# Attention and SoLU kernel, first stage: sums of squares as Gram products, low words shifted by ScalarE, the first strided values loaded to both places

## The chip, the cores and the metric

The kernel runs on one core of a Trainium2 chip. The metric is the device time of one execution in microseconds (us); lower is better. Of the kernel before, the median of three runs is 548.46 us (547.02 to 554.54). One further execution was recorded with the hardware profiler: it took 552.05 us, and its span, from which all times "at x us" below are counted, is 550.3 us.

## The reference

An attention over 8 batches of 8 heads, 576 positions and 64 channels, and behind it a SoLU layer (512 to 1024 to 512) on the 4608 tokens.

```python
mask_local = (rel >= 0) & (rel < 32)                               # heads 0 to 3
mask_strided = (rel >= 0) & (pos[None] % 32 == pos[:, None] % 32)  # heads 4 to 7
attn = softmax(where(masks, q @ k.T / sqrt(64), -1e9)) ; x = attn @ v
h = x @ w_in                                       # 4608x512 @ 512x1024
solu = h * softmax(h)
ln = (solu - mean(solu)) / sqrt(var(solu) + 1e-6) * g_ln
return ln @ w_out                                  # 4608x1024 @ 1024x512
```

`q`, `k`, `v` and `g_ln` are 32-bit floats; `w_in` and `w_out` arrive as 64-bit floats, that is as two 32-bit words for each number.

## The kernel before, in words

**Attention.** Each batch has five units: two of the strided heads (`UNITS` 0 and 1; the positions are laid out so that each residue modulo 32 is a block of 18) and three of the local heads. A unit `n` makes scores on TensorE (L385 adds the mask by a product with the unit matrix, L390 is q times k), takes maximum, difference, exponential and sum (L396 to L400), scales with the reciprocal on GpSimd (L408), splits the result into two half-precision parts in `p` (L414 on ScalarE, L415 on VectorE), turns `p` by a DMA transpose into `pt` (L417) and multiplies with the values (L439) into `x_ps`. The product is again split into two parts, `xhi` and `xlo` (L455, L456), rings that hold two batches.

**Values.** `vloc` and `vstr` of a batch are loaded (L322) and their squares summed by ScalarE (`v_scale`, L329). A product with ones (L298) adds over the partitions, and from the total a power of two is made (L302 to L308, in `pow2_scale`). `v_split` (L344, L345) makes two half-precision parts; seven DMAs (L360) copy them to where the products need them, four of them for the strided values (`vd`, in both halves of the partitions) and three for the local ones (`ve`).

**Weights.** Once, ahead of the layer: `decode` loads a piece of 512 numbers of a weight row (L565), takes the high word through ScalarE (Prelu, L568), shifts the low word right by 29 on VectorE (L571) and joins the two (L572). There are 16 such pieces, 8 of `w_in` and 8 of `w_out`. ScalarE sums their squares (L584, L605), `pow2_scale` makes a scale, and each weight is split into two half-precision parts: for `w_in` the upper one by ScalarE (L591), the lower one by TensorE (a product with `wdiag`, L595, less one with `minus`, L597) and a copy (L599); for `w_out` by L618 and L619.

**Layer.** A token tile is 128 tokens, 36 in all. `ff` has two halves of the first product, each of 12 matmuls of 512 columns (`g1`, L497 to L499, into `h_ps`), then maximum (L504), exponential (L515), product (L518), centring (L522, L523), squares (L525), a short chain on GpSimd (L529 to L533), a DMA transpose of `c` into `ct` (L536), and two halves of the second product (`g2`, L541 to L543). The result goes out by L549 and L550.

**Order.** Every step is given to `Plan.add` with its engine, an assumed duration, what it reads and writes, and a key. `Plan.order` simulates the engines with these durations and writes the instructions out in the order it finds; where several steps are ready, the lowest key goes first. Keys stand in tables (`UK`, `PK` for units, `TK`, `GK` for token tiles, and so on). On the chip each engine then works its instructions strictly in the order written; SP issues nearly all DMAs, and a DMA that waits holds up those behind it on SP. One key serves the whole weight preparation (`KW`, `KO`). The rooms for raw weight words are the idle layer buffers `e`, `u` and four `room` tiles of 1024 words.

## Time and profile before

| | |
|---|---|
| median of three runs | 548.46 us (547.02 to 554.54) |
| the profiled execution | 552.05 us; span 550.3 us |
| TensorE busy | 476.1 us, 87% of the span |
| VectorE busy | 367.3 us, 67% |
| ScalarE busy | 301.0 us, 55% |
| GpSimd busy | 135.0 us, 25% |
| DMA | 96.89 MB moved, mean 176 GB/s |
| first matmul of the layer (L497) starts | at 62.28 us |
| first matmul of the second product (L541) starts | at 91.25 us |

In the profile PE is TensorE, PEld its weight loads, DVE VectorE, ACT ScalarE, POOL GpSimd, SP the engine that issues DMAs. A row of a timeline has the start, the duration, the engine, the line, the operation and the tiles (written, then read). Rows of waits say which engine waited at which line for whom, with the total, the number and the longest.

### The profile page before, as it was taken

Reading aid. Unit: us, or ns where it says so; the run is one execution under the profiler, and the core shown is the slowest. Engines: PE = TensorE matmul, PEld = TensorE weight load, DVE = VectorE, ACT = ScalarE, POOL = GpSimd, SP = SyncE. Lnnn points to the kernel's source line nnn. Section 1 sums busy time; section 2 is a strip of 40 time slices with the busy share of each in tenths; the row PEclk is TensorE's granted clock in tenths of the full one; section 3 lists DMA queues with packets and bytes.
Section 4 is the critical chain, followed back from the end, with each engine's and each line's share of the span. In section 5 each row is a group of like instructions: output and inputs, shape, how many; then the busy total and the mean of one; then the engine's idle time right before and its main releaser. Section 6 shows DMA issues by size and latency. Waiting matters only on the chain.

```text
span 550.3 us, 11771 instructions
## 1 busy us (share of the span) xinstructions
PE 476.1 (87%) x4770; PEld 240.5 (44%) x4770; DVE 367.3 (67%) x705; ACT 301.0 (55%) x445; POOL 135.0 (25%) x247
## 2 busy tenths in 40 slices
PE   0264778979998999999899899699999899998996
PEld 0231434445444455455444454344455455544442
DVE  3777879748874589647955679436966679635440
ACT  4877846564554756546646556624556556525441
POOL 3011024402351124303421233202241235211120
PEclk9999689999999999999999999889999999999999
DMA  8999587979993299999793399939994397644441
GB/s 304 409 277 274 151 176 168 192 161 211 228 217 69 57 245 240 227 198 196 203 196 77 105 223 202 217 91 236 214 195 109 85 217 160 117 86 59 96 96 57
DMA packets 171158, 96.89 MB, mean 176 GB/s; under 512 B 138208, under 2 KB 157280, under 8 KB 171104
## 3 DMA queue, kind: packets, MB, share of 16 engines
q1 hardware_dynamic: 165920, 86.71, 74.5%
q10 hardware_dynamic: 5184, 9.44, 5.7%
q8 instruction: 37, 0.61, 0.5%
q14 instruction: 17, 0.14, 0.1%
HBM read 39.24 MB, written 9.44 MB: 88 GB/s over the span
## 4 chain that ended last, share of the span: by engine, by line
PE 65%; DVE 14%; DMA 9%; ACT 5%; issue 5%; SPq 1%; POOL 0%; DVEq 0%; ACTq 0%
PE h_ps L497 10%; PE h_ps L499 10%; PE h_ps L498 10%; PE o_ps L541 8%; PE o_ps L542 8%; PE o_ps L543 8%; DVE u L518 4%; DMA ct<-c 4%; PE s_ps L390 3%; PE x_ps L439 3%; DVE st L504 3%; DMA room<-w_out 2%; DMA vrs<-vstr 2%; DMA q<-qloc 2%; DVE c L523 1%
## 5 line engine op out<-in xcount | busy, mean ns | idle before, releaser
L497 PE MATMUL h_ps<-w,xhi 128*128 128x512 f16 x280 | 107.2, 383 | 15.7 <-DVE u L518 13.3
L541 PE MATMUL o_ps<-obuf,ct 128*128 128x512 f16 x272 | 104.4, 384 | 9.2 <-DMA ct<-c 8.3
L499 PE MATMUL h_ps<-w,xlo 128*128 128x512 f16 x280 | 107.1, 383 | 0.6 <-DVE xlo L456 0.5
L498 PE MATMUL h_ps<-w,xhi 128*128 128x512 f16 x280 | 107.1, 382 | 0.0
L542 PE MATMUL o_ps<-obuf,ct 128*128 128x512 f16 x272 | 104.0, 382 | 0.0
L543 PE MATMUL o_ps<-obuf,ct 128*128 128x512 f16 x272 | 103.8, 382 | 0.0
L408 POOL TENSOR_TENSOR t<-t,m 128x576 f32<-128x576 f32 (+2 forms) x40 | 50.2, 1255 | 179.0 <-DVE m L405 128.1
L518 DVE SCALAR_TENSOR_TENSOR u<-h_ps,st,e 128x1024 f32<-128x1024 f32 x35 | 44.6, 1275 | 42.0 <-ACT e L515 26.7
L504 DVE TENSOR_REDUCE st<-h_ps 128x1 f32<-128x1024 f32 x35 | 42.6, 1218 | 43.6 <-PE h_ps L499 43.6
L515 ACT ACTIVATE e<-h_ps,st,vsc 128x1024 f32<-128x1024 f32 x31 | 37.3, 1205 | 57.2 <-DVE st L505 21.5
L522 ACT ACTIVATE c<-u,st 128x1024 f16<-128x1024 f32 x36 | 41.3, 1148 | 38.5 <-DVE st L521 36.5
L523 DVE SCALAR_TENSOR_TENSOR c<-u,st,c 128x1024 f16<-128x1024 f32 x36 | 47.1, 1309 | 18.2 <-ACT c L522 18.0
L531 POOL TENSOR_SCALAR st<-st 128x1 f32<-128x1 f32 x36 | 21.5, 597 | 112.8 <-ACT junk L525 111.8
L498 PEld LDWEIGHTS <-xhi 128*128 128x128 f16 x288 | 28.3, 98 | 46.7 <-issue 17.9
L541 PEld LDWEIGHTS <-ct 128*128 128x128 f16 x288 | 28.2, 98 | 44.0 <-DMA ct<-c 8.5
L390 PE MATMUL s_ps<-k,q 64*54 64x54 f32 (+1 forms) x1280 | 41.3, 271 | 5.8 <-DMA k<-kstr 5.8
L499 PEld LDWEIGHTS <-xlo 128*128 128x128 f16 x288 | 28.2, 98 | 36.9 <-DVE xlo L456 2.9
L543 PEld LDWEIGHTS <-ct 128*128 128x128 f16 x288 | 28.4, 98 | 34.7 <-issue 1.1
L414 ACT CAST p<-t 128x576 f16<-128x576 f32 (+2 forms) x40 | 26.9, 672 | 29.6 <-POOL t L408 29.2
L542 PEld LDWEIGHTS <-ct 128*128 128x128 f16 x288 | 28.3, 98 | 32.6 <-issue 3.0
L399 ACT ACTIVATE t<-t 128x576 f32<-128x576 f32 (+2 forms) x40 | 27.4, 685 | 27.3 <-DVE t L397 26.0
L497 PEld LDWEIGHTS <-xhi 128*128 128x128 f16 x288 | 28.2, 98 | 32.3 <-issue 0.6
(136 smaller groups left out, 706.9 us busy)
## 6 DMA issues: line engine op xcount, KB each, us to landing
out<-ob ACTq DMA_DIRECT2D x36, 256.0 KB, 3.2
vrs<-vstr SPq DMA_DIRECT2D x8, 768.0 KB, 7.8
vd<-vs SPq DMA_DIRECT2D x16, 384.0 KB, 9.3
vrl<-vloc SPq DMA_DIRECT2D x8, 640.0 KB, 6.0
q<-qstr SPq DMA_DIRECT2D x8, 594.0 KB, 5.0
k<-kstr SPq DMA_DIRECT2D x8, 594.0 KB, 6.6
q<-qloc SPq DMA_DIRECT2D x8, 576.0 KB, 4.2
k<-kloc SPq DMA_DIRECT2D x8, 576.0 KB, 5.7
```

Of the source, the lines that this page charges most:

```text
L390: nc.tensor.matmul(s_ps[row : row + nq, pair, i * nk : (i + 1) * nk], q_raw[half][hs, q0 : q0 + (nq - 1) * nqb + 1 : nqb], k_raw[half][hs, ...
L408: add("pool", nx * nk / 510 + 0.02, lambda: nc.gpsimd.tensor_tensor(tv, tv, sm.unsqueeze(2).broadcast_to([P, nx, nk]), op=ALU.mult), key + ...
L497: nc.tensor.matmul(hv[:, i], xhi[:, cc, tok], whi[:, cc, cols], start=(cc == 0), stop=False)
L498: nc.tensor.matmul(hv[:, i], xhi[:, cc, tok], wlo[:, cc, cols], start=False, stop=False)
L499: nc.tensor.matmul(hv[:, i], xlo[:, cc, tok], whi[:, cc, cols], start=False, stop=(cc == 3))
L504: add("dve", 1.21, lambda: nc.vector.tensor_reduce(low, hv, axis=AX.XY, op=ALU.max, negate=True), key + 0.2, r=HH, w=[(ST, "low")])
L518: add("dve", 1.3, lambda: nc.vector.scalar_tensor_tensor(uv, hv, ia, ev, op0=ALU.mult, op1=ALU.mult, accum_out=us), key + 0.3, r=[*HH, E, ...
L522: add("act", 1.2, lambda: nc.scalar.activation(c[:, 0], u, AF.Identity, bias=mean, scale=1.0), key + 0.35, r=[U, (ST, "mean")], w=[(C, 0)])
L523: add("dve", 1.28, lambda: nc.vector.scalar_tensor_tensor(c[:, 1], u, mean, c[:, 0], op0=ALU.add, op1=ALU.subtract), key + 0.4, r=[U, (ST, ...
L541: nc.tensor.matmul(o, ct[:, cc, :], ohi[:, cc, :], start=(cc == 0), stop=False)
L542: nc.tensor.matmul(o, ct[:, cc, :], olo[:, cc, :], start=False, stop=False)
L543: nc.tensor.matmul(o, ct[:, 8 + cc, :], ohi[:, cc, :], start=False, stop=(cc == 7))
```

## The change

It concerns what is done once, ahead of the layer and for batch 0 and 1.

- The squares of `w_in`, of `w_out` and of the values of batch 0 are no longer summed by ScalarE. `gram` multiplies each block of 128 columns by itself on TensorE (the upper 16 bits of each number, read as bf16), 98 products of 128 columns in all (34 for the values, 32 for `w_in`, 32 for `w_out`); VectorE takes the diagonal's sum (L314 of the new kernel). For `w_out` the largest square of `g` takes the place of each row's own, by two small products and three small VectorE operations.
- `decode` works on pieces of 1024 numbers, eight in all. The low word's shift is now a ScalarE operation (L630), no longer one of VectorE. The loads are of twice the size. `e` and `u` become one tile, the four rooms two.
- The lower part of the weights is made by TensorE and a copy for two of the four pieces of `w_in`, by VectorE (L648) for the other two. `wdiag` is made on GpSimd.
- The strided values of batch 0 are loaded twice, once into partitions 0 to 63 and once into 64 to 127 (`vtwo`), so that `v_split` writes `vd` itself (two operations on ScalarE, two on VectorE) and the four DMAs of L360 go for this batch. In later batches the two halves of `vtwo` hold what `vrs` and `vs` held.
- For batches 0 and 1 the lower part of `p` is made by GpSimd, no longer by VectorE.
- `w_out` is loaded behind the transposes of units 1 and 2. Each single step of this stage has a key of its own (`SK`), and all tables are new.

On SP, which issues the loads, the program before begins with these rows, from the third DMA on (`room`, `e`, `u` and `ct` are rooms for raw weight words):

```order
L322 DMA vrl_72<-vloc 128x1280
L565 DMA e_107<-w_in 128x1024
L565 DMA e_106<-w_in 128x1024
L565 DMA u_109<-w_in 128x1024
L322 DMA vrs_73<-vstr 128x1536
L261 DMA mask_86<-masks 128x288
L565 DMA u_108<-w_in 128x1024
L565 DMA room_70<-w_in 128x1024
L565 DMA room_68<-w_in 128x1024
L565 DMA ct_114<-w_out 128x1024
L317 DMA q_64<-qstr 128x1188
L318 DMA k_66<-kstr 128x1188
```

The changed program begins on SP with these, from the first DMA on:

```order
L272 DMA mask_83<-masks 128x288
L352 DMA q_64<-qstr 128x1188
L353 DMA k_66<-kstr 128x1188
L361 DMA vtwo_72<-vstr 64x2x1536 x2
L626 DMA eu_103<-w_in 128x2048
L365 DMA vrl_70<-vloc 128x1280
L626 DMA room_67<-w_in 128x2048
L352 DMA q_63<-qloc 128x1152
L353 DMA k_65<-kloc 128x1152
L695 DMA g_124<-g 128x8
L626 DMA room_68<-w_in 128x2048
L626 DMA eu_104<-w_in 128x2048
```

The mask and the strided q and k moved from behind the weights to the front, the strided values come twice, and no `w_out` is among the first loads. The next rows on SP load the strided q and k of batch 1, then comes the transpose of unit 0, the two value loads of batch 1, the first `ve` copy, the transpose of unit 1, the other two `ve` copies, the transpose of unit 2, and then the first `w_out`.

On ScalarE, the last rows before the first product of the layer were these (`obuf` is `w_out`, L455 writes `xhi` of units 0, 1 and 2):

```order
L605 ACTIVATE ob_115,o_sc_128<-obuf_126 128x512
L455 CAST xhi_104<-x_ps 128x2x18x18
L568 ACTIVATE obuf_126<-room_67 128x512
L414 CAST p_99<-t_93 128x6x96
L329 ACTIVATE junk_71,vm_79<-vrl_72 128x1280
L605 ACTIVATE ob_116,o_sc_128<-obuf_126 128x512
L329 ACTIVATE junk_71,vm_79<-vrs_73 128x1536
L455 CAST xhi_104<-x_ps 128x2x18x15
L618 ACTIVATE obuf_126<-obuf_126,gg_131 128x512 x2
L455 CAST xhi_104<-x_ps 128x2x192
```

In the changed program the rows there are these (L646 and L660 are the upper and lower parts of `w_in`, L403 a value split of batch 1, L518 writes `xhi` of units 1 and 2, L629 is the first step on `w_out`):

```order
L646 ACTIVATE w_120<-c_105,w_sc_122 128x1024
L518 CAST xhi_101<-x_ps 128x2x18x15
L646 ACTIVATE w_120<-ct_108,w_sc_122 128x1024
L403 ACTIVATE vtwo_72<-vtwo_72,vsc_80 128x1536
L660 CAST w_120<-h_ps 128x512
L646 ACTIVATE w_120<-c_106,w_sc_122 128x1024
L518 CAST xhi_101<-x_ps 128x2x192
L646 ACTIVATE w_120<-ct_107,w_sc_122 128x1024
L660 CAST w_120<-h_ps 128x512
L629 ACTIVATE obuf_121<-room_68 128x1024
L459 ACTIVATE t_87<-t_87 128x576
L660 CAST w_120<-h_ps 128x512 x2
```

Before, `w_in` was split well ahead, and all of `w_out` stood before the first product of the layer; now the split of `w_in` stands directly before it, and `w_out` but for one step behind it. On TensorE the first product of the layer stands behind the values' products of units 0, 1 and 2 in both programs; the total of the squares of `w_in` (L332) stands behind the values' product of unit 1 in the new one.

The diff, cut to its core:

```diff
@@ new: sums of squares on TensorE
+    def gram(dst, pieces, key, w, room, scrap):
+        acc, A = room
+        for i, (x, r) in enumerate(pieces):
+            def products(i=i, x=x):
+                y = x.bitcast(BF16).rearrange("p (f t) -> p f t", t=2)
+                n = x.shape[1]
+                for f in range(0, n, P):
+                    z = y[:, f : f + P, 1]
+                    nc.tensor.matmul(acc, z, z, start=(i == 0 and f == 0), stop=(i == len(pieces) - 1 and f == n - P))
+            add("pe", 0.11 * x.shape[1] / P + 0.1, products, key(), r=r, w=[A])
+        scrap, J = scrap
+        add("dve", 0.35, lambda: nc.vector.scalar_tensor_tensor(scrap, acc, 2.0 ** (-2 * SQ), unit_sb, op0=ALU.mult, op1=ALU.mult, accum_out=dst),
+            key(), r=[A, "unit"], w=[J, w])
@@ load_v, batch 0, strided
+                def twice(i=i):
+                    nc.sync.dma_start(vtwo[i * D : i * D + D].rearrange("p (y f) -> p y f", y=2), vstr[b].rearrange("(y p) f -> p y f", y=2))
@@ v_split, batch 0, strided
+            for y in range(2):
+                hi, lo = vd_sb[:, 0, :, y], vd_sb[0:D, 1, :, y]
+                add("act", 1.55, lambda y=y, hi=hi: nc.scalar.mul(hi, raw[:, :, y], sc[:, 1:2]), k(), r=R, w=[("v2", 1, y)])
+                add("dve", 1.8, lambda y=y, hi=hi, lo=lo: nc.vector.scalar_tensor_tensor(lo, raw[0:D, :, y], sc[0:D, 1:2], hi[0:D], op0=ALU.mult, op1=ALU.subtract),
+                    k(), r=[*R, ("v2", 1, y)], w=[("v2", 1, 2 + y)], lock=True)
@@ unit, lower part of p
-        add("dve", w + 0.15, lambda: nc.vector.tensor_tensor(lo, tv, hi, op=ALU.subtract), key + 0.45, r=[T, PB], w=[PB], lock=True)
+        if b < POOL_LO:
+            add("pool", nx * nk / 510 + 0.02, lambda: nc.gpsimd.tensor_tensor(lo, tv, hi, op=ALU.subtract), key + 0.45, r=[T, PB], w=[PB])
@@ decode
-        add("sp", 1.26, lambda: nc.sync.dma_start(raw, src.rearrange("p (f t) -> p f t", t=2)), LW[n], w=RAW, dma=LOAD)
+        add("sp", 2.52, lambda: nc.sync.dma_start(raw, src), LW[n], w=RAW, dma=LOAD, after=after)
-            nc.vector.tensor_scalar(w0, w0, 29, None, op0=ALU.logical_shift_right)
+        add("act", 1.15, lambda: nc.scalar.activation(w0, w0.bitcast(U32), AF.Identity, bias=nhalf, scale=2.0**-29 - 2.0**-49), sk(), r=[*RAW, "consts"], w=RAW)
@@ prep_w
-            add("act", 1.15, lambda cc=cc: nc.scalar.activation(ob_sb[cc % 2].bitcast(BF16), stage[cc], AF.Square, scale=2.0**-SQ,
+        gram(w_sc[:, 4:5], [(flat[cc], ST[cc]) for cc in range(4)], sk, "wm", (h_ps[:, 0, 0:P], ("h", 0)), (ob_sb[1][:, 0 : P // 2].bitcast(BF16), ("ob", 1)))
+            if cc >= 2:
+                add("dve", 1.28, lambda hv=hv, wv=wv, lv=lv: nc.vector.scalar_tensor_tensor(lv, wv, w_sc[:, 1:2], hv, op0=ALU.mult, op1=ALU.subtract), sk(),
@@ prep_o
-        for cc in range(8):
-            decode(o32[:, cc], w_out[cc * P : (cc + 1) * P, :], key, ("od", cc), O_ROOMS[cc], 8 + cc)
+        for i in range(4):
+            decode(dst, w_out[2 * i * P : (2 * i + 2) * P].rearrange("(c p) (f t) -> p c f t", c=2, t=2), D2, ROOMS[(i + 2) % 4], 4 + i,
+                   [turned[AFTER_O[i]]])
+        gram(gm[:, 3:4], pieces, sk, "om0", (o_ps[:, 0:P], "o"), (ob_sb[0][:, 0 : P // 2].bitcast(BF16), ("ob", 0)))
@@ tables (all new; the first row of one)
-    -38.84, -36.52, -39.37, -9.95, -7, -2.09, -2.44, 1, 2.8, 9.53, 4.72, 5.21, 6.19, 26.76, 7.83, 13.91, -1.33, 5.79, 9.98, 13.84, 14.31, 15.8, 15.06,
+    -0.75, -1.19, -22.37, -7, -8.68, 1.9, -27.44, -3.1, 31.53, 1.96, 6.34, 18.79, 1.12, 8.18, 10.46, 11.55, 9.13, 11, 9.39, 12.11, 13.78, 11.22, 17.5,
```

More of the change, by code (lines that the diff above doesn't have):

```diff
@@ L155, in order @@
                         break
-                end = dma_free + lands + self.LATE
+                end = dma_free + lands + (LATE0 if steps[n][6] == LOAD and now < 20 else self.LATE)
             else:
@@ L295, in part_sum @@
                 nc.vector.tensor_reduce(one, parts, axis=AX.X, op=ALU.add)
-        add("dve", 0.17, part_sum, key, r=r, w=[(w, "one")])
-        add("pe", 0.15, lambda: nc.tensor.matmul(tot, ones, one, start=True, stop=True), key, r=["ones", (w, "one")], w=[T])
+        if parts.shape[1] > 1:
+            add("dve", 0.17, part_sum, key(), r=r, w=[(w, "one")])
+            r = [(w, "one")]
+        else:
+            one = parts.bitcast(BF16)[:, 1:2]
+        add("pe", 0.15, lambda: nc.tensor.matmul(tot, ones, one, start=True, stop=True), key(), r=["ones", *r], w=[T])
         def root():
@@ L321, in load_v @@
     def load_v(b, a, key):
+        if b == 0 and a:
+            for i in range(2):
+                def twice(i=i):
+                    nc.sync.dma_start(vtwo[i * D : i * D + D].rearrange("p (y f) -> p y f", y=2), vstr[b].rearrange("(y p) f -> p y f", y=2))
+                add("sp", 1.95, twice, key, w=[("vr", 1), ("v", 1, 0), ("v", 1, 1)] if i == 0 else [("vr2", 1)], dma=LOAD)
+            return
         add("sp", (1.57, 1.93)[a], lambda: nc.sync.dma_start(vr_sb[a], (vloc, vstr)[a][b]), key, w=[("vr", a)], dma=LOAD)
@@ L325, in v_scale, with square @@
         vm, sc = vm_sb[b % 2], vsc_sb[b % 4]
[L326 to L332 removed]
+        k = sk if b == 0 else lambda: key
+        if b == 0:
+            gram(vm[:, 0:1], [(vtwo, [("vr", 1), ("vr2", 1)]), (vr_sb[0], [("vr", 0)])], k, ("vm", 0, 0), (o_ps[:, 0:P], "o"), (junk[:, 0:P], "junk"))
+            n = 1
+        else:
+            n = 2
+            for a in range(2):
+                def square(a=a):
+                    w = vr_sb[a].shape[1]
+                    nc.scalar.activation(junk[:, 0:w], vr_sb[a], AF.Square, scale=2.0**-SQ, accum_out=vm[:, a : a + 1])
+                add("act", (1.36, 1.58)[a], square, k(), r=[("vr", a)], w=["junk", ("vm", b % 2, a)])
+        pow2_scale(sc, vm[:, 0:n], vs1_sb[b % 2], k, [("vm", b % 2, a) for a in range(n)], ("vsc", b % 4),
+                   (o_ps[:, P : P + 1], "o") if b == 0 else (s_ps[:, 1, 511:512], ("s", 1)), 8, 1.0 / P_SCALE)
         def hscale():
@@ L561, in decode @@
+    def decode(dst, src, w, room, n, after=()):
         room, RAW = room
-        raw = room.rearrange("p (f t) -> p f t", t=2)
-        w0, w1 = raw[:, :, 0], raw[:, :, 1]
+        raw = room.rearrange("p c (f t) -> p c f t", t=2)
+        w0, w1 = (raw[:, :, :, t].rearrange("p c f -> p c f") for t in range(2))
         di = dst.bitcast(I32)
-        add("sp", 1.26, lambda: nc.sync.dma_start(raw, src.rearrange("p (f t) -> p f t", t=2)), LW[n], w=RAW, dma=LOAD)
-        add("act", 0.67, lambda: nc.scalar.activation(dst, w1.bitcast(F32), AF.Prelu, scale=2.0**-112, alpha=-(2.0**32)), key, r=RAW, w=[w])
@@ L584, in prep_w @@
-            add("act", 1.15, lambda cc=cc: nc.scalar.activation(ob_sb[cc % 2].bitcast(BF16), stage[cc], AF.Square, scale=2.0**-SQ,
-                                                                accum_out=w_sc[:, 4 + cc : 5 + cc]), key,
-                r=ST[cc], w=[("wm", cc), ("ob", cc % 2)])
-        pow2_scale(w_sc, w_sc[:, 4:8], s1_sb[:, 0:1], key, [("wm", cc) for cc in range(4)], "w_sc", (h_ps[:, 0, 0:1], ("h", 0)))
-        add("dve", 0.2, lambda: nc.vector.tensor_scalar(wdiag, unit_sb, w_sc[:, 1:2], None, op0=ALU.mult), key, r=["w_sc", "unit"], w=["wdiag"])
```

173 lines of the change are left out of this document (96 added, 77 removed), and 4 rows, old and new, of the table SK.

## The prediction

> **What bounds the kernel now.** I read the slices of the page first, then busy time by stretch, then whom TensorE waited for, then the timeline where those waits lie.
>
> ```profile
> PE   0264778979998999999899899699999899998996
> PEclk9999689999999999999999999889999999999999
> ```
>
> From the eighth slice on TensorE is busy nearly throughout; what it loses, it loses in the first slices. The stretches put numbers to it (columns: stretch, its length, then busy time and count of PE, PEld, DVE, ACT, POOL, then granted clock, DMA share, GB/s). I cut them at the first matmul of the layer's first product and at the first of its second product:
>
> ```profile
> 0.00:62.28 62.28, 23.15 (x332) 13.92 (x332) 42.00 (x95) 45.38 (x78) 9.73 (x31) 0.93 0.98 293
> 62.28:91.24 28.96, 23.87 (x272) 11.74 (x268) 24.67 (x45) 15.59 (x23) 6.15 (x9) 0.91 0.73 183
> 91.24:140.00 48.76, 44.99 (x491) 23.07 (x489) 36.01 (x66) 26.56 (x39) 14.97 (x23) 1.00 1.00 188
> 140.00:520.00 380.00, 359.50 (x3578) 180.91 (x3576) 258.81 (x492) 204.77 (x295) 100.68 (x174) 0.99 0.80 163
> ```
>
> TensorE stands idle for 39.1 us before 62.28, 5.1 us up to 91.24, 3.8 us up to 140, and 20.5 us in the 380 us after. In the first stretch DMA is at a share of 0.98, ScalarE and VectorE at 73% and 67%: no one engine bounds it, a chain does. Of the first 140 us:
>
> ```profile
> PE s_ps L298 <- DVE vs L295: 17.5, 2, 16.5
> PE x_ps L439 <- DMA pt<-p: 6.5, 1, 6.5
> ...
> PE h_ps L497 <- DVE u L518: 4.6, 2, 2.8
> ```
>
> and where it lies:
>
> ```profile
> 23.20 1.50 PE L390 MATMUL s_ps<-k,q 64*54 64x54 f32 x48 [5.79 <-DMA k<-kstr]
> ...
> 24.64 0.19 PE L298 MATMUL h_ps<-s,ones 128*128 128x1 bf16 x1
> ...
> 26.55 0.16 DVE L306 RECIPROCAL w_sc<-w_sc 128x1 f32<-128x1 f32 x1
> ...
> 56.37 1.27 PE L439 MATMUL x_ps<-pt,vd 118*64 118x54 f16 x40 [6.46 <-DMA pt<-p]
> ...
> 62.28 0.61 PE L497 MATMUL h_ps<-w,xhi 128*128 128x512 f16 x1
> ```
>
> The first scores wait for k until 23.20, unit 1's product with the values waits for its transpose until 56.37, and the layer's first matmul starts at 62.28. From there on the work left for TensorE sets the end. So the change is worth what it moves that 62.28, plus TensorE work it adds behind it, less waits it takes away there.
>
> **When the first matmul of the layer would start.** I follow the DMA queue of SP, in its new order. Rate and sizes:
>
> ```profile
> 4.16 10.46 DMA vrs<-vstr
> ```
>
> ```profile
> 10.00:20.00 10.00, 0.65 (x5) 0.26 (x4) 7.25 (x20) 7.11 (x13) 0.00 (x0) 1.00 1.03 411
> 33.00:38.00 5.00, 5.00 (x32) 2.13 (x34) 3.48 (x6) 1.92 (x5) 0.00 (x0) 1.00 1.24 180
> ```
>
> ```profile
> vrs<-vstr SPq DMA_DIRECT2D x8, 768.0 KB, 7.8
> ...
> vrl<-vloc SPq DMA_DIRECT2D x8, 640.0 KB, 6.0
> q<-qstr SPq DMA_DIRECT2D x8, 594.0 KB, 5.0
> ...
> q<-qloc SPq DMA_DIRECT2D x8, 576.0 KB, 4.2
> ...
> room<-w_in SPq DMA_DIRECT2D x4, 512.0 KB, 7.9
> ...
> mask<-masks SPq DMA_DIRECT2D x1, 144.0 KB, 10.2
> ```
>
> The strided values landed at 14.62 (4.16 and 10.46) behind five weight pieces of 512 KB and 640 KB of local values: 3968 KB, 4.06 MB, 9.9 us at 411 GB/s. So the stream starts at 4.7 us. In the new order mask, q and k (k has q's shape) are 1332 KB, which land at 8.0 us against 23.20. All through the last `w_in` piece are 8760 KB (with twice 768, four times 1024, 640 and four loads of local q and k and `g`), 8.97 MB: 26.5 us. Batch 1's strided q and k, 1.22 MB, make 29.5. Then come the transpose of unit 0 (12x128x128 half-precision numbers, 0.39 MB), two value loads of batch 1 (1408 KB, 3.5 us), a `ve` copy of 0.33 MB, and the transpose of unit 1 (0.33 MB). In the second row, from 33 to 38 us, copies inside SBUF (`vd` and `ve`) were under way, at 180 GB/s; at that the transposes take an estimated 2.2 and 1.8 us and the copy 1.8 us, which leads to 38.8 us. To the landing I add 1.4, the least landing of a transpose in the first 110 us less its own 2.2:
>
> ```profile
> DMA to landing us min/median/max: 3.6/5.9/10.4
> ```
>
> That is 40.2 where the trace of before has 56.37. Unit 1's product takes 1.27; the total of the `w_in` squares stands behind it, and from that product to the finished scale took 2.1 us (24.64 to 26.71): 43.6. Now ScalarE has a row of twelve instructions in front of the first layer matmul, with these prices:
>
> ```profile
> L591 ACT ACTIVATE w<-c,w_sc 128x1024 f16<-128x1024 f32 x2 | 2.2, 1133 | 0.0
> ...
> L344 ACT ACTIVATE vs<-vrs,vsc 128x1536 f16<-128x1536 f32 x1 | 1.6, 1561 | 0.0
> ...
> L599 ACT CAST w<-h_ps 128x512 f16<-128x512 f32 x8 | 4.6, 592 | 3.2 <-PE h_ps L595 2.7 <-PE h_ps L597 0.5
> L568 ACT ACTIVATE obuf<-room 128x512 f32<-128x512 f32 x5 | 3.2, 674 | 3.1 <-DMA room<-w_out 3.1
> L399 ACT ACTIVATE t<-t 128x576 f32<-128x576 f32 (+2 forms) x4 | 2.8, 696 | 0.6 <-DVE t L397 0.6
> ...
> L455 ACT CAST xhi<-x_ps 128x648 f16<-128x648 f32 (+2 forms) x3 | 1.7, 577 | 0.0
> ```
>
> Four upper parts 4.5, two `xhi` 1.2, a value split 1.6, three copies 1.8, one word conversion of twice the size 1.3, one exponential 0.7: 11.1 us, and a start at 54.7, which is 7.6 us earlier. The removed squares and shifts are not subtracted anywhere: they are beside this chain, and what they free is already in the row of twelve.
>
> One price has no row: a load of 64 partitions from memory, twice 768 KB. At 411 GB/s both take 3.8 us, as assumed above. The nearest row is that of 33 to 38 us, when by the order of issue the `vd` and `ve` copies moved, whose targets are 64 partitions or fewer: 180 GB/s at a DMA share of 1.24, so the queue was full and the rate less than half. The other bound is thus 8.7 us. Those copies come from SBUF, some in runs of 512 bytes, so I take half of 411 rather than 180: 7.7 us, 3.9 us later for all behind, and a start at 58.6, **3.7 us earlier** than before. By the Trainium skill, page "SBUF — State Buffer", section "Door 1: The DMA port swizzle", partitions 0 to 63 reach only 8 of the 16 ports, and two transfers to the two halves hardly run faster together than one after the other; by it the two loads would take an estimated 7.2 us. The row of 33 to 38 us agrees in direction; that no load from memory to 64 partitions stands in the trace remains.
>
> **What is behind that start.** Of the 98 products of 128 columns only the 32 for `w_out` lie behind it; the other 66 and the halved L595 and L597 lie in 39.1 us of idle time, which hides them. No such product is in the trace. Bounds: 31 ns, as the 48 small ones at 23.20 in 1.50 us, and 383 ns, a layer matmul of four times the columns:
>
> ```profile
> L497 PE MATMUL h_ps<-w,xhi 128*128 128x512 f16 x280 | 107.2, 383 | 15.7 <-DVE u L518 13.3
> ...
> L541 PEld LDWEIGHTS <-ct 128*128 128x128 f16 x288 | 28.2, 98 | 44.0 <-DMA ct<-c 8.5
> ```
>
> Each needs its own weight load, so I take that load's 98 ns: 32 of them, **+3.1 us** (1.0 to 12.3). The first scores of batch 1 have moved ahead of the start: **-1.5 us**, by the row at 23.20.
>
> Between first and second product TensorE waited 4.6 us for L518, the longer wait 2.8 us, and behind that the clock fell:
>
> ```profile
> 78.00:80.00 2.00, 2.00 (x6) 0.65 (x5) 2.00 (x3) 2.00 (x3) 0.00 (x0) 0.50 0.11 39
> ```
>
> In the new order the `w_out` products and two scores stand where that wait was, so I let the 2.8 go, and 1.0 for two microseconds at half clock: **-3.8 us** (0 to -5.6). VectorE is what is waited for there, with 24.67 of 28.96 us. It gets four joins of `w_out` of twice the size and gives up about five lower parts of `p`:
>
> ```profile
> L572 DVE SCALAR_TENSOR_TENSOR obuf<-obuf,room 128x512 int32<-128x512 int32 x5 | 4.3, 856 | 0.3
> L408 POOL TENSOR_TENSOR t<-t,m 128x576 f32<-128x576 f32 (+2 forms) x40 | 50.2, 1255 | 179.0 <-DVE m L405 128.1
> ...
> L415 DVE TENSOR_TENSOR p<-t,p 128x576 f16<-128x576 f32 (+2 forms) x40 | 30.9, 773 | 7.3 <-ACT p L414 7.2
> ```
>
> That is +6.8 us at twice 856, at most (pieces elsewhere run at 692), against -3.9 us: VectorE is not relieved there, which is why I don't let all waits go. GpSimd takes the lower parts at about the 1.26 us of L408; busy 6.15 of 28.96 us, it has room, but each `p` is done 0.5 us later, and the transpose behind it on SP holds up the loads after it by as much.
>
> **The sum**, against the profiled execution of 552.05 us (span 550.3): -3.7 +3.1 -1.5 -3.8 = -5.9, so 546.15. That execution is 3.6 us above the median of 548.46; the same taken off gives **542.5 us**.
>
> **The rivals.**
>
> *The loads to 64 partitions run at the full rate*, and all of the 5.6 us of waits and half clock goes: 552.05 -7.6 +1.6 -5.6 = 540.45, on the median's footing 536.9. For it speaks that the loads are long runs from memory, unlike the copies; against it the 180 GB/s.
>
> *`w_out` comes too late in the queue.* Its 4096 KB are 10.2 us at 411 GB/s. Before, they were through by 36 us; now they stand behind the transpose of unit 2, in the stretch in which also the `vd` copies of batch 1, four more transposes of `p` and the first of `c` queue up. TensorE works its rows in order and stops at the `w_out` products, or at the second product for want of `ct`. In the stretch from 62.28 to 91.24 the DMA share was 0.73, so 7.8 us were free; the rival decides from the point where more than that comes, and costs up to the full 10.2 us if the gaps can't be used because each transpose waits for GpSimd: 546.15 + 10.2, on the median's footing 552.8, slower than before. Against it: four `vd` copies of batch 0 are gone from the queue.
>
> *All tables are new, so stalls far behind may come or go.* The largest:
>
> ```profile
> PE o_ps L541 <- DMA ct<-c: 5.0, 1, 5.0
> ```
>
> It lies behind 140 us. Gone, the sum is 537.5; a second of its kind makes 547.5. Nothing in the trace says which.
>
> **Chances.** The forecast 0.50, full rate 0.25, late `w_out` 0.15, stalls far behind 0.10. The range, 533 to 553 us, reaches from a little below the full rate (it may come with a stall gone) to the late `w_out`, and holds the bounds of the products' price. The forecast's own range is 538 to 548. About 2%, 11 us, is what a measurement of this kernel can tell from no change (the three runs spread by 7.5 us): faster means below 537.5, slower above 559.4. Faster by over 2% are about half of the full-rate case, a part of the forecast's own lower tail and of the stalls gone: 0.28. Slower by over 2% needs a late `w_out` and a further stall: 0.07. Within 2%: 0.65.
>
> **What would show it.** First scores near 8 us; unit 1's product with the values at 40 to 44 us; the first layer matmul at 55 (full rate) to 59 us (half). While the strided values load, the rate shows which: near 411 or near 200 GB/s. The `w_out` products should be near 0.1 us each. If the late `w_out` holds, TensorE's waits name a DMA of `w_out` or `ct` ahead of the second product; if the wait for L518 stays, the 3.8 us were wrong. The forecast is wrong as a whole if the layer starts at 59 us or earlier and the end moves by less than that.

## The result, and the profile after

| | before | changed |
|---|---|---|
| median | 549.86 us (547.02 to 554.54, 4 runs) | 530.88 us (528.67 to 533.22, 4 runs) |
| the profiled execution | 552.05 us, span 550.3 us | 528.67 us, span 527.0 us |
| TensorE busy | 476.1 us | 476.0 us |

The ratio is 0.965 (95% interval 0.957 to 0.973): **faster by 3.5%**, where 542.5 us, 1.1% below the median before, had been forecast, and outside the range of 533 to 553 us. A later series of six runs of the same kernel gave 531.07 us and 0.968 (0.962 to 0.974).

In these two executions TensorE is busy for as long as before, so the 23.3 us between their spans are all time in which it stood idle. (The medians differ by 19.0 us; the profiled execution lies 2.2 us above the median before and 2.2 us below the median of the changed kernel.) The two slice rows of the page of the changed kernel that answer to those of before:

```profile
PE   1547969989999999989999899999998999989996
PEclk9857998999999999999999999999999999999999
```

The early slices are fuller, but so are some in the middle. To see how much lies where, I cut both executions at the same places of the work: at the first matmul of the layer (token tile 0), and at the first matmul of the token tiles 12 and 22. Busy time by stretch of the kernel before (stretch, its length, busy time and count of PE, PEld, DVE, ACT, POOL, granted clock, DMA share, GB/s):

```profile
0.00:62.30 62.30, 23.17 (x333) 13.94 (x334) 42.02 (x95) 45.40 (x78) 9.73 (x31) 0.93 0.98 293
62.30:216.77 154.47, 141.41 (x1499) 71.98 (x1496) 116.40 (x220) 85.92 (x125) 40.80 (x68) 0.98 0.85 176
216.77:365.39 148.62, 137.98 (x1433) 69.49 (x1432) 97.49 (x182) 81.35 (x117) 41.95 (x67) 0.98 0.90 182
365.39:550.30 184.91, 173.58 (x1516) 85.03 (x1514) 111.41 (x210) 88.34 (x128) 42.50 (x81) 1.00 0.64 132
```

and of the changed kernel:

```profile
0.00:53.33 53.33, 26.14 (x440) 19.23 (x441) 35.34 (x69) 33.45 (x39) 18.31 (x36) 0.78 1.04 307
53.33:207.02 153.69, 144.63 (x1540) 74.66 (x1537) 118.22 (x223) 94.97 (x135) 54.84 (x75) 0.99 0.93 197
207.02:342.80 135.78, 132.78 (x1401) 67.69 (x1399) 93.51 (x185) 79.11 (x116) 40.43 (x66) 1.00 0.87 188
342.80:527.00 184.20, 172.48 (x1489) 84.55 (x1485) 112.20 (x204) 86.74 (x127) 40.23 (x81) 1.00 0.61 132
```

The lengths differ by -9.0, -0.8, **-12.8** and -0.7 us. The largest of these lies in tiles 12 to 21. That stretch begins over 150 us behind the layer's first matmul, 120 us behind the last split of `w_out` (L686, at 86.42 us) and 80 us behind the last lower part of `p` that the edit gives to GpSimd (L476, at 125.92 us). TensorE's idle time (length less its busy time) was 39.1, 13.1, 10.6 and 11.3 us; it is 27.2, 9.1, 3.0 and 11.7. So half of the idle time that went lay ahead of the layer, a third in tiles 12 to 21. The length of that stretch fell by more than its idle time because 5.2 us of TensorE's busy time left it too. Twelve matmuls of the second product (it has 265 instead of 277), 0.22 us each from start to start, now lie in other stretches (2.6 us), and ten that came at half clock behind the wait for `ct` below, 0.43 us from start to start at a granted 0.50, no longer do (2.1 us).

How much of such a difference is scatter, a second profiled execution of the same changed kernel shows (run 12 below, 534.81 us, span 533.1 us), cut at the same places:

```profile
0.00:54.73 54.73, 26.54 (x440) 19.55 (x440) 35.16 (x69) 33.38 (x39) 18.33 (x36) 0.78 1.05 303
54.73:213.16 158.43, 147.33 (x1540) 75.87 (x1537) 119.56 (x227) 94.82 (x135) 56.11 (x76) 0.97 0.91 193
213.16:348.93 135.77, 132.76 (x1401) 67.66 (x1399) 92.33 (x180) 79.14 (x116) 38.46 (x65) 1.00 0.89 186
```

Tiles 12 to 21 repeat to 0.01 us. But the start moves by 1.4 us and tiles 0 to 11 by 4.7 us between two executions of one kernel, so against this one the differences are -7.6, +4.0, -12.9 and -0.7 us. What a single execution shows in the first two stretches can't be read finer than that. (The sixth run, which has the order of before up to about 220 us, starts the layer at 63.16 us and takes 152.34 us for tiles 0 to 11, so the earlier start is clear of it.)

The waits of TensorE in tiles 12 to 21, first before (all that name a wait of over 0.5 us), then changed (the only one):

```profile
PE o_ps L541 <- DMA ct<-c: 5.0, 1, 5.0
PE h_ps L497 <- DVE u L518: 3.0, 3, 1.4
PE s_ps L298 <- DVE vs L295: 1.4, 1, 1.4
PE s_ps L385 <- DVE t L397: 0.8, 1, 0.8
```

```profile
PE s_ps L332 <- DVE vs L325: 3.0, 3, 1.4
```

The timeline of the changed kernel up to its first layer matmul (L450 are scores, L332 the total of squares, L340 the finished scale of `w_in`, L646 its first upper part, L502 unit 1's product with the values, L560 the layer):

```profile
6.89 1.41 PE L450 MATMUL s_ps<-k,q 64*54 64x54 f32 x44 [1.83 <-DMA k<-kstr]
...
14.78 1.44 PE L310 MATMUL o_ps<-vtwo 128*128 128x128 bf16 x12 [6.38 <-DMA vtwo<-vstr]
...
40.21 0.16 PE L332 MATMUL h_ps<-w_sc,ones 128*128 128x1 bf16 x1 [0.39 <-DVE ob L314]
...
40.79 0.17 DVE L340 RECIPROCAL w_sc<-w_sc 128x1 f32<-128x1 f32 x1
41.66 1.15 ACT L646 ACTIVATE w<-c,w_sc 128x1024 f16<-128x1024 f32 x1
42.24 1.27 PE L502 MATMUL x_ps<-pt,vd 118*64 118x54 f16 x40 [1.87 <-DMA pt<-p]
...
53.31 0.39 PE L560 MATMUL h_ps<-w,xhi 128*128 128x512 f16 x1
```

The scores start at 6.89 us (23.20 before), unit 1's product at 42.24 (56.37), the layer at 53.31 (62.28). The total at 40.21 waited for the diagonal of the Gram products alone, and stands **ahead** of unit 1's product. The text before the prediction says that it stands behind it, and the prediction builds on that. What stands behind it, at 43.45, is another instruction of the same line, the total of the values of batch 1.

### The profile page after: what moved, and what is told of

Its sections match the earlier page's. It is cut to its first block, busy times and chain, and to the rows that moved or that the text cites. A ratio compares the mean times of both kernels' runs of the same rounds, so it can differ in the third digit from the quotient of the medians.

```text
span 527.0 us, 11895 instructions
## 1 busy us (share of the span) xinstructions
PE 476.0 (90%) x4858; PEld 246.1 (47%) x4858; DVE 359.3 (68%) x679; ACT 294.3 (56%) x414; POOL 153.8 (29%) x258
## 4 chain that ended last, share of the span: by engine, by line
PE 74%; DVE 12%; DMA 5%; issue 4%; ACT 3%; POOL 1%; SPq 0%; ACTq 0%; DVEq 0%; POOLq 0%
PE h_ps L560 12%; PE h_ps L562 11%; PE h_ps L561 11%; PE o_ps L604 9%; PE o_ps L605 8%; PE o_ps L606 8%; PE s_ps L450 4%; PE x_ps L502 4%; DVE st L567 3%; DVE eu L581 3%; DMA vtwo<-vstr 2%; DMA pt<-p 2%; PE s_ps L445 1%; PE h_ps L656 1%; DMA ct<-c 1%
## 5 line engine op out<-in xcount | busy, mean ns | idle before, releaser
L560 PE MATMUL h_ps<-w,xhi 128*128 128x512 f16 x280 | 107.0, 382 | 8.8 <-DVE eu L581 5.7
L468 POOL TENSOR_TENSOR t<-t,m 128x576 f32<-128x576 f32 (+2 forms) x40 | 52.3, 1309 | 135.8 <-DVE m L465 106.1
L581 DVE SCALAR_TENSOR_TENSOR eu<-h_ps,st,eu 128x1024 f32<-128x1024 f32 x35 | 44.8, 1280 | 40.7 <-PE h_ps L562 19.2
L585 ACT ACTIVATE c<-eu,st 128x1024 f16<-128x1024 f32 x36 | 41.3, 1147 | 41.2 <-DVE st L584 39.5
L578 ACT ACTIVATE eu<-h_ps,st,vsc 128x1024 f32<-128x1024 f32 x31 | 37.3, 1204 | 47.8 <-DVE st L568 22.1
L586 DVE SCALAR_TENSOR_TENSOR c<-eu,st,c 128x1024 f16<-128x1024 f32 x36 | 45.9, 1276 | 22.1 <-ACT c L585 22.1
L594 POOL TENSOR_SCALAR st<-st 128x1 f32<-128x1 f32 x36 | 23.5, 653 | 120.9 <-ACT junk L588 120.0
L606 PEld LDWEIGHTS <-ct 128*128 128x128 f16 x288 | 28.2, 98 | 34.0
L560 PEld LDWEIGHTS <-xhi 128*128 128x128 f16 x288 | 28.3, 98 | 32.7 <-issue 0.8
L450 PE MATMUL s_ps<-k,q 64*54 64x54 f32 (+1 forms) x1280 | 41.1, 270 | 2.7 <-DMA k<-kstr 1.8
L605 PEld LDWEIGHTS <-ct 128*128 128x128 f16 x288 | 28.2, 98 | 31.7 <-issue 2.2
L450 PEld LDWEIGHTS s_ps<-k,q 64*54 64x54 f32 (+1 forms) x1280 | 39.5, 198 | 3.3 <-issue 3.3
```

The source lines that it names most:

```text
L450: nc.tensor.matmul(s_ps[row : row + nq, pair, i * nk : (i + 1) * nk], q_raw[half][hs, q0 : q0 + (nq - 1) * nqb + 1 : nqb], k_raw[half][hs, ...
L468: add("pool", nx * nk / 510 + 0.02, lambda: nc.gpsimd.tensor_tensor(tv, tv, sm.unsqueeze(2).broadcast_to([P, nx, nk]), op=ALU.mult), key + ...
L560: nc.tensor.matmul(hv[:, i], xhi[:, cc, tok], whi[:, cc, cols], start=(cc == 0), stop=False)
L581: add("dve", 1.3, lambda: nc.vector.scalar_tensor_tensor(uv, hv, ia, ev, op0=ALU.mult, op1=ALU.mult, accum_out=us), key + 0.3, r=[*HH, E, ...
L585: add("act", 1.2, lambda: nc.scalar.activation(c[:, 0], u, AF.Identity, bias=mean, scale=1.0), key + 0.35, r=[U, (ST, "mean")], w=[(C, 0)])
L586: add("dve", 1.28, lambda: nc.vector.scalar_tensor_tensor(c[:, 1], u, mean, c[:, 0], op0=ALU.add, op1=ALU.subtract), key + 0.4, r=[U, (ST, ...
```

## The experiments

Twelve runs. Two things were to be told apart: what of the gain comes from the first stage, and what from the new key tables far behind it; and in the first stage, which of its parts carries it. Theory A puts the gain in the middle of the program on the new key tables, theory B on the first stage; later theories are named where they come up. Each ratio is against runs of the kernel before on the same chip.

### 1 and 2: the late order of the one in the other

"Late" are all steps of batches 2 to 7 and of token tiles 9 to 35. The planner is put aside, and the steps are written out by a list: those of the first stage as the kernel has them, the late ones in the relative order of the other kernel.

```diff
-    for n in plan.order():
+    for n in ORDER:      # first run: changed kernel, late steps in the order of before
         plan.steps[n][2]()
```

> The changed kernel, but every step of batches 2 to 7 and of token tiles 9 to 35 stands in the relative order that it had in the kernel before; the first stage is as changed. Theory A (9.2 of the 23.2 us of span were won in the 380 us behind the first stage, because the new tables put the later rows in an order with fewer stalls): TensorE's idle time behind 116.7 us goes back from 16.7 us to about 26, and the time is 538 to 542 us. Theory B (the later stalls went because the first stage hands over earlier and with more work in hand): idle time behind 116.7 us stays at 15 to 19 us and the time at 529 to 533 us.

> The kernel before, but every step of batches 2 to 7 and of token tiles 9 to 35 stands in the relative order of the changed kernel. Theory A: idle time of TensorE behind 140 us falls from 26 us to about 17, and the time is 538 to 542 us. Theory B: it stays at 23 to 28 us, and the time at 546 to 551 us.

Measured: the changed kernel with the old late order 546.14 us (ratio 0.992, 0.988 to 0.996); the kernel before with the new late order 557.86 us (1.015, 1.009 to 1.021). Both times lie outside both theories. The stretches from tile 0 to 12 and from 12 to 22 show why, first for the first run, then for the second:

```profile
53.03:210.91 157.88, 144.38 (x1480) 73.92 (x1476) 114.79 (x220) 93.69 (x133) 50.19 (x74) 0.97 0.82 183
210.91:358.60 147.69, 138.36 (x1433) 69.47 (x1432) 97.57 (x182) 81.38 (x117) 41.85 (x67) 0.98 0.87 184
```

```profile
61.79:236.09 174.30, 150.03 (x1559) 75.34 (x1556) 119.00 (x223) 87.21 (x127) 43.23 (x69) 0.95 0.80 167
236.09:371.87 135.78, 132.77 (x1401) 67.67 (x1399) 93.52 (x185) 79.14 (x116) 40.41 (x66) 1.00 0.92 187
```

Tiles 12 to 21 take 135.78 us with the new late order, to the hundredth as in the changed kernel, although all before them is the old kernel; with the old late order they take 147.69 us, near the old 148.62, although all before them is new. What that stretch takes hangs on its own order and not on the first stage. But where early and late steps meet, in tiles 0 to 11, an order that was not made for this first stage can cost: 174.30 us instead of 154.47 in the second run, more than the gain behind it. In the first run no such cost is shown: its 157.88 us lie within the 153.69 and 158.43 us that the changed kernel itself took there.

### 3: the strided values at full rate

An extra input holds the strided values of batch 0 twice, so that two loads into all 128 partitions bring what two loads into 64 partitions each brought. The order is untouched.

```diff
-  nc.sync.dma_start(vtwo[i * D : i * D + D]..., vstr[b].rearrange("(y p) f -> p y f", y=2))
+  nc.sync.dma_start(vtwo[:, i * w : i * w + w], v2[:, i * w : i * w + w])   # v2: the same numbers, laid out twice
```

> The changed kernel, in which the strided values of batch 0 come laid out twice in memory and are loaded by two transfers of 128 partitions, no longer two of 64; the order is unchanged. If the half rate (212 to 215 GB/s from 7 to 13 us) is what delays the first stage, the values land 3 to 3.5 us earlier, the first layer matmul starts at 50 us, no longer 53.3, and the time falls by 3 us. If the chain of ScalarE and VectorE between 19 and 53 us sets the start, the values land as much earlier, the start moves by less than 1.5 us and the time by less than 1.5 us.

The DMA rate while these values load, in the changed kernel:

```profile
7.00:9.00 2.00, 1.40 (x48) 1.23 (x48) 0.55 (x1) 0.00 (x0) 0.00 (x0) 1.00 1.07 215
9.00:11.00 2.00, 0.00 (x0) 0.00 (x0) 1.16 (x3) 0.74 (x1) 0.00 (x0) 1.00 0.98 215
11.00:13.00 2.00, 0.00 (x0) 0.00 (x0) 1.19 (x3) 0.00 (x0) 0.59 (x1) 1.00 1.07 212
```

and at that place in the third run:

```profile
5.00:7.00 2.00, 0.26 (x12) 0.23 (x11) 0.00 (x0) 0.00 (x0) 0.52 (x3) 1.00 1.04 386
7.00:9.00 2.00, 1.38 (x49) 1.21 (x46) 0.64 (x1) 0.00 (x0) 0.00 (x0) 1.00 0.97 387
```

212 to 215 GB/s into 64 partitions, 386 to 387 into all of them, at an equally full queue: the half rate of the forecast is shown. By the Trainium skill, page "SBUF — State Buffer", section "Door 1: The DMA port swizzle", 64 neighbouring partitions reach half of the ports; the rates agree. The time was 527.43 us (ratio 0.960, 0.955 to 0.964), 3.5 us below the 530.9 of the changed kernel by the medians (1.3 by the spans of the profiled executions), with the layer starting at 51.28 instead of 53.33 or 54.73. The slowest of its four executions, 528.16 us, is below the fastest of the changed kernel's ten, 528.57. This version beats both kernels, at the price of an input laid out twice.

### 4: the lower parts of `p` back on VectorE

```diff
-  add("pool", ..., lambda: nc.gpsimd.tensor_tensor(lo, tv, hi, op=ALU.subtract), ...)
+  add("pool", ..., lambda: nc.vector.tensor_tensor(lo, tv, hi, op=ALU.subtract), ...)   # batches 0, 1; place in the order kept
```

> The changed kernel, in which the lower parts of p of batches 0 and 1 are made by VectorE again, at the same places of the order. If GpSimd's part relieves VectorE, the first stage gets longer by half of the 7.7 us that VectorE takes on: a start of the layer at 55 to 57 us and 533 to 535 us. If what VectorE is spared comes back as waiting (joins of 1.6 to 2.2 us, where 1.19 is their time undisturbed, and lower parts on GpSimd of 1.7 to 2.2 us against 0.77 on VectorE), the time is within 1.5 us of the changed kernel's 530.9 us.

530.49 us (0.965, 0.960 to 0.970): no difference. What one such operation takes, on GpSimd in the changed kernel and on VectorE in this run, in the first 90 us:

```profile
L476 POOL TENSOR_TENSOR p<-t,p 128x576 f16<-128x576 f32 x4 | 6.9, 1713 | 3.6 <-ACT p L474 3.4 <-issue 0.2
```

```profile
L476 DVE TENSOR_TENSOR p<-t,p 128x576 f16<-128x576 f32 x4 | 3.0, 760 | 0.0
```

GpSimd takes 1.71 us, over twice as long. The 4.0 us of VectorE (363.3 less 359.3 us busy) that it buys are worth nothing that this run can show.

### 5 and 6: change of order in mid-work

The same kind of list, but the late steps change from the one relative order to the other only at a place at about 220 us, where both orders have done all but eight of the same steps.

```diff
-    for n in plan.order():
+    for n in ORDER:      # fifth run: changed kernel, order of before from about 220 us on; sixth: the reverse
```

> The changed kernel; from the place in the plan that lies at about 220 us on (the two orders have there done all but eight of the same steps), the steps of the later batches and token tiles stand in the relative order of the kernel before. Up to that place nothing differs from the changed kernel. Theory A (the order that the tables give behind 220 us is worth 5 to 6 us by itself, as TensorE's idle time in 200 to 500 us says: 14.9 us in the kernel before and 15.0 in the changed kernel with the old late order, 9.3 and 9.8 with the new one): 536 to 537 us. Theory C (the order behind 220 us is worth nothing by itself; the gain lies in a first stage and an order of the next 150 us that fit each other): 530 to 532 us.

> The counterpart: the kernel before; its own order up to the place at about 220 us, the order of the changed kernel from there on. Theory A: 549.5 less 5.5, so 543.5 to 545 us. Theory C: 548.5 to 551 us, as the kernel before.

The fifth run took 537.47 us (0.981, 0.978 to 0.985), near the 536 to 537 us of theory A: some 6.5 us are lost by the order behind alone. The sixth took 547.54 us (0.999, 0.996 to 1.002), no faster than before, as theory C has it. TensorE's idle time, from the windows cut at tiles 0, 12 and 22 as above, shows where they differ:

| run | to tile 0 | 0 to 11 | 12 to 21 | behind |
|---|---|---|---|---|
| before | 39.1 | 13.1 | 10.6 | 11.3 |
| changed | 27.2 | 9.1 | 3.0 | 11.7 |
| 1: changed, old late order | 27.3 | 13.5 | 9.3 | 11.8 |
| 2: before, new late order | 39.4 | 24.3 | 3.0 | 11.7 |
| 5: changed, old order from 220 us | 27.4 | 12.3 | 8.9 | 11.8 |
| 6: before, new order from 220 us | 40.0 | 11.3 | 7.7 | 11.8 |
| 12: changed, once more | 28.2 | 11.1 | 3.0 | 11.7 |

The changed kernel, run 5 and run 12 have one order up to about 220 us: what differs in their first two columns is scatter. In the sixth run the changeover lies in the stretch from tile 12 on, and with it that stretch has 7.7 us of idle time where the whole new order has 3.0: much of what the new order brings there is taken back. That explains a part only. In the profiled execution the two stretches from tile 12 on are together 5.0 us shorter than before (144.27 and 184.23 us), while the medians differ by 0.7 us; where the rest is lost is open.

### 7 and 8: the squares of one weight back on ScalarE

At the places of the Gram products, ScalarE sums the squares again, and VectorE adds up the four sums in place of the diagonal; only the engines and the operations change, not the place in the order.

```diff
             def products(i=i, x=x):
+                if sq is not None:     # seventh run: w_in; eighth run: w_out
+                    nc.scalar.activation(ob_sb[1].bitcast(BF16), x, AF.Square, scale=2.0**-SQ, accum_out=sq[:, i : i + 1])
+                    return
```

> The changed kernel, its order kept, with one part undone: the squares of w_in are summed by ScalarE again (four passes over 128x1024 with their read of the sum, by the squares of token tiles in the changed kernel 1.14 + 0.19 us each, 5.3 us together), at the places in the program where TensorE's Gram products of w_in stood. Theory S (ScalarE's row sets the start of the layer): ScalarE idles 0.84 + 1.00 + 1.39 = 3.2 us between 24 and 41 us, so the layer's first matmul comes at 55.4 to 58.6 us instead of 53.3, and the time is 533 to 536 us. Theory D (VectorE, GpSimd and the loads set the start, ScalarE has room): first matmul within 1 us of 53.3, time 530 to 532 us.

> The changed kernel, its order kept, with the squares of w_out on ScalarE again (four passes of 128x1024, 5.3 us) at the places of the Gram products of w_out; TensorE is spared 32 products of 78 ns, 2.5 us, in 60 to 67 us. Theory S: ScalarE idles 3.4 us between 55 and 70 us, so about 2 us of delay of what follows on it (the move of the first token tiles' gated halves at 64.98, 69.69 and the split of w_out from 77.5), and 531 to 533 us. Theory T (TensorE is the bound there): 528 to 530 us.

Seventh run: 532.07 us (0.971, 0.967 to 0.974), eighth: 533.26 us (0.975, 0.970 to 0.979). Against 531.07 us (0.968) of the changed kernel in run 12 that is 1.0 and 2.2 us more; by the ratios, since the chips differ, it is about 1.5 and 3.7 us, and all these intervals overlap with that of run 12. The stretch up to the layer and its first matmul in the seventh run, and the wait that grew in the eighth (up to 90 us; in the changed kernel 1.4 us in two waits):

```profile
0.00:54.79 54.79, 23.24 (x408) 16.76 (x408) 35.09 (x68) 37.32 (x47) 16.86 (x36) 0.75 1.02 323
```

```profile
54.78 0.39 PE L571 MATMUL h_ps<-w,xhi 128*128 128x512 f16 x1
```

```profile
PE h_ps L571 <- DVE eu L592: 4.3, 1, 4.3
```

The seventh run's start at 54.79 us, between its two theories, is not to be told from the changed kernel's own 53.33 and 54.73. What changed ahead of it is that TensorE is spared its products (23.24 us busy instead of 26.14 and 26.54) and idles the longer for it (31.55 us instead of 27.19 and 28.19). The Gram products of the weights are a small part of the gain.

### 9 and 10: the late keys alone, planned anew

Here the tables themselves are exchanged: the entries of batches 2 to 7 and of tiles 9 to 35, and the planner makes its order from them.

```diff
-TK = [-2.79, 3.02, 17.91, 0.94, 1.94, 6.18, 9.3, 11.79, 11.84, 7.52, 12.09, ...]
+TK = [-2.79, 3.02, 17.91, 0.94, 1.94, 6.18, 9.3, 11.79, 11.84, 1.22, 13.11, ...]   # ninth run: first nine as changed, the rest of before
```

> The changed kernel with one part of it undone in the tables themselves: the key numbers of batches 2 to 7 and of token tiles 9 to 35 are those of the kernel before; the planner plans anew, so its order may fit the place where early and late steps meet. Theory A (the late keys are worth what TensorE's idle time behind token tile 15 says: 21.2 us in the kernel before, 14.8 in the changed one): 530.9 + 6.4 = 536 to 539 us if the planner closes the gap at the meeting, 541 to 546 if the meeting costs what it cost in the second and the sixth run (5 to 8 us). Theory D (the late keys matter little once the plan is made anew): 530 to 533 us.

> The counterpart: the kernel before with the late key numbers of the changed kernel, planned anew. Theory A: 549 - 6.4 = 541 to 544 us if the meeting costs nothing, 547 to 552 if it costs 5 to 8 us. Theory D: 548 to 550 us.

The ninth run, the changed first stage with the old late keys, took 543.00 us (0.990, 0.986 to 0.994); the tenth, the old first stage with the new late keys, 543.49 us (0.990, 0.987 to 0.994). Tiles 12 to 21 of the ninth and of the tenth:

```profile
208.12:352.83 144.71, 133.50 (x1421) 67.90 (x1419) 96.74 (x184) 81.33 (x117) 39.87 (x67) 1.00 0.88 180
```

```profile
216.83:355.86 139.03, 134.04 (x1452) 68.47 (x1448) 98.47 (x191) 80.81 (x119) 41.26 (x65) 1.00 0.92 193
```

Planned anew, that stretch takes neither the 148.62 us of before nor the 135.78 us of the changed kernel. By the medians each half is worth about 6 us by itself, 6.5 for the first stage with its single steps and 6.0 for the late keys; both together are worth 19, and the remaining 6 us come only when the late keys and the first stage belong together. The ninth run's 6.5 us lie near the 5.9 us that the prediction had summed for a first stage with nothing changed behind it, but that is luck: in its profiled execution the layer starts 9.5 us earlier than before (52.78 instead of 62.30), tiles 0 to 11 take 0.9 us more, and tiles 12 to 21 take 3.9 us less. That execution's span of 538.1 us is 12 us below that of before, but the median of its nine runs lies 3 us above the profiled one; where the others lose that is open.

### 11: the low words' shift back on VectorE

```diff
-  nc.scalar.activation(w0, w0.bitcast(U32), AF.Identity, bias=nhalf, scale=2.0**-29 - 2.0**-49)
+  nc.vector.tensor_scalar(w0, w0, 29, None, op0=ALU.logical_shift_right)     # same place in the order
```

> The changed kernel, its order kept, with the shift of the low words back on VectorE (tensor_scalar, 2 x 0.42 us by the kernel before, against 1.24 us on ScalarE), at the same places in the program: VectorE gets 8 x 0.84 = 6.7 us more in 15 to 66 us, ScalarE is spared 8 x 1.24 = 9.9 us. Theory V (VectorE is on the path of the first stage): the layer's first matmul 2 to 4 us later than 53.3 and 533 to 535 us. Theory S (ScalarE's row is the path): 1 to 3 us earlier, 528 to 530 us.

The shifts on VectorE, and the stretch up to the layer:

```profile
L630 DVE TENSOR_SCALAR room<-room 128x1024 int32<-128x1024 int32 x4 | 3.8, 956 | 0.3 <-DMA room<-w_in 0.3
L630 DVE TENSOR_SCALAR eu<-eu 128x1024 int32<-128x1024 int32 x4 | 3.7, 930 | 4.4 <-DMA eu<-w_in 4.4
```

```profile
0.00:54.62 54.62, 26.53 (x440) 19.37 (x440) 37.95 (x72) 29.02 (x35) 17.54 (x36) 0.75 1.00 297
```

534.98 us (0.973, 0.969 to 0.977), 4 us more than the changed kernel by the medians and 3 us by the ratios, as theory V has it in the time and against theory S, which had it faster. Where they are lost is not shown: its start at 54.62 us (the theory had 2 to 4 us more than 53.3) and its tiles 0 to 11 at 155.72 us, cut in the same way, lie between the changed kernel's two executions. VectorE was 37.95 us busy ahead of the start where it had 35.34, while ScalarE's 4.4 us of relief (29.02 instead of 33.45) bought nothing; that VectorE is the tighter engine of the two in the first stage fits this, but is argued from it.

### 12: the changed kernel again

> The changed kernel itself, unedited, in five rounds: the base against which the single undone parts are read (four runs of it so far gave 0.9647 of the kernel before, 0.9565 to 0.973). Theory A and every other here: 529 to 533 us, 0.961 to 0.970. Were it 0.973 or more, the parts undone in runs seven, eight and eleven (0.9707, 0.9747, 0.9734) would not differ from it.

531.07 us (0.968, 0.962 to 0.974). By the medians the eleventh run lies 3.9 us above it, the eighth 2.2, the seventh 1.0; by the ratios 3.0, 3.7 and 1.5. The intervals overlap in all three, so that the parts of the first stage can be ranked from these runs only roughly: undone one at a time, each of the four (runs 4, 7, 8 and 11) costs between nothing and 4 us. The mask, q and k moved to the front, the doubled load of the strided values, the larger pieces and the steps' own keys were not undone one by one; what share they have in the first stage's gain is open.

## Why the prediction was wrong

**What was right.** The scores were forecast for 8.0 us and came at 6.89. The half rate of the loads to 64 partitions was chosen from a row of 180 GB/s that spoke of other copies, and came at 212 to 215. Unit 1's product was put at 40 to 44 us and came at 42.24, 1.9 us ahead of the 44.1 that the working gives with the half rate. That TensorE's idle time sets the end held too: its busy time changed by 0.1 us in the two executions compared.

**The step that failed first: the chain from unit 1's product to the layer.** The prediction put one behind the other, from 44.1 us on, the product (1.27 us), the total of the `w_in` squares with its scale (2.1) and ScalarE's row of twelve (11.1), in all 14.5 us. In the trace it is 11.07 us from the product to the layer (42.24 to 53.31). The total stands ahead of the product; the scale was done at 40.96, and the row began at 41.66, where the prediction had 47.5. These 3.4 us and the 1.9 us above make the 5.3 us by which the start undercut the forecast 58.6. The order of the total and the product was there to be read from the changed program's rows on TensorE.

Nor was ScalarE's row what filled those 11.07 us. TensorE itself was busy for 10.39 of them: beside the products of units 1 and 2 and two sets of scores it worked the products that make the lower parts of `w_in`, L656 and L657 (L595 and L597 before), which the prediction had put into idle time that hides them.

```profile
43.49 2.05 PE L656 MATMUL h_ps<-c,wdiag 128*128 128x512 f32 x2
45.34 0.63 PE L657 MATMUL h_ps<-w,minus 128*128 128x512 f16 x1
...
50.59 1.12 PE L656 MATMUL h_ps<-c,wdiag 128*128 128x512 f32 x2 [0.68 <-ACT w L660]
51.55 0.38 PE L657 MATMUL h_ps<-w,minus 128*128 128x512 f16 x1
51.86 0.33 PE L445 MATMUL s_ps<-mk_str,unit 64*64 64x324 bf16 x4
52.02 1.35 PE L450 MATMUL s_ps<-k,q 64*54 64x54 f32 x48
```

The only gap is the 0.68 us for ScalarE's copy; behind the last L657 come the first scores of batch 1, and directly behind those, without a wait, the layer. ScalarE's row ran beside this, 9.87 us busy from 41.66 to the end of its twelfth instruction near 52.6, and stood still twice for TensorE (0.75 and 0.35 us). That the row was put at 11.1 us and the layer began 11.65 us behind its start is thus luck in part.

**The step that failed most: the rival of the stalls far behind.** It was named, with the right wait (`ct` waiting for the transpose of `c`, 5.0 us), but as a coin to be tossed: ±5 us, at a chance of 0.10, with the forecast itself at "nothing changes there". The stretch of tiles 12 to 21 gave 12.8 us, and in the seven other runs that have the whole of the new late order (2, 3, 4, 7, 8, 11 and 12) it takes 135.77 to 135.80 us, whatever the first stage does. Of this, 7.6 us are idle time that went, 5.0 of them that wait; the rest is TensorE time: 137.98 us busy became 132.78, at a granted clock of 1.00 instead of 0.98 and with 32 matmuls fewer in the stretch. With the 2.1 us of half clock behind it that one wait cost 7.1 us; about 2.6 us, the twelve matmuls of the second product, moved elsewhere and are no gain. The "nothing" of the forecast should have been a term with bounds: between 91 and 520 us TensorE was idle for 24.3 us in the rows that the prediction quotes (3.8 and 20.5), the most of it that new tables could take away.

**The smaller terms.** The 32 products for `w_out` cost 78 ns each, 2.5 us, where 98 ns and 3.1 us were put; the row over the first 90 us:

```profile
L310 PE MATMUL o_ps<-obuf 128*128 128x128 bf16 x32 | 2.5, 220 | 0.8 <-DVE obuf L631 0.8
```

(The 220 ns are the time from issue to end of one; they overlap, and together they keep TensorE busy for 2.5 us.) The wait for VectorE's product with `h` fell from 4.6 to 2.4 us in the first 140 us, by 2.2 where 2.8 were put; the half clock, put at 1.0 us, did not go (granted 0.83 between 80 and 90 us); and the waits of a unit's product for `xlo` grew from 0.9 to 3.2 us. The length of tiles 0 to 11 changed by -0.8 us (by +4.0 in run 12), where the three terms that lay there made -2.2 (+3.1, -1.5, -3.8).

**The rivals.** The late `w_out` did not happen: TensorE named `w_out` once, for 0.8 us (the row above). The premise that all of it was loaded by 36 us before was wrong: the last of the eight pieces was issued at 44.23 us. The full rate, by the third run, is worth 3.5 us, near the 3.9 us put on it.

**The sum put right.** -9.0 for the start, -0.8 for tiles 0 to 11, -12.8 for tiles 12 to 21, -0.7 behind, together -23.3 of span. With the start as measured the forecast would have been 537 us, still 6 us too high: the larger miss is the table.

## What to carry to other kernels

Where an order is planned from tables and the tables change for the whole program, cut the profile of before at fixed places of the work and give each stretch's idle time a term of its own in the sum, up to all of it; "far behind the edit" is no reason for zero. Take a second profile of the same kernel before reading small differences between stretches: here two executions differed by 4.7 us in one stretch and by 0.01 us in another. An early edit and the order behind it can be worth less apart than together: here 6.5 and 6.0 us apart and 19 together, and an order made for another beginning can cost more than the edit brings. For the place of one step relative to another, read the order on the engine itself, not the order in which the steps are added.
